# Memory attention and two MoE layers: the next batch's phi, k and v work woven into a batch's softmax, V W_in behind it

## The chip, the cores and the metric

One core of one Trainium2 chip runs the kernel. The metric is the device time of one launch in microseconds. The core's engines each run their own list of instructions in order: TensorE (PE, with its weight loads as PEld), VectorE (DVE), ScalarE (ACT) and GpSimd (POOL) compute, SyncE (SP) issues nearly all DMAs. An engine whose next instruction waits lets everything behind it in its list wait.

## What is computed

Eight batches of 8 heads, 576 tokens, head size 64 and 32 memory slots; then two dense layers over the 4608 tokens of 512 numbers.

```python
a = phi - np.max(phi, axis=2, keepdims=True)        # over the tokens
a = np.exp(a); a = a / (np.sum(a, axis=2, keepdims=True) + 1e-09)
k_m = np.einsum('bhsm,bhsd->bhmd', a, k)
v_m = np.einsum('bhsm,bhsd->bhmd', a, v)
scores = scale * np.matmul(q, k_m.transpose(0, 1, 3, 2))
attn = softmax(scores)                              # over the 32 slots
x = heads_side_by_side(np.matmul(attn, v_m))        # 4608 x 512
h = x @ w_in;  x = (h - np.tanh(h)) @ w_out         # 512 -> 2048 -> 512
h = np.maximum(np.maximum(x @ w1, x @ w2), x @ w3)  # 512 -> 768
out = h @ w_out2                                    # 768 -> 512
```

## The kernel before, in words

**Stages.** The first layer goes in two passes (ph 0 and 1) over the 2048 hidden columns, 1024 in each; a third stage does the second layer. Attention is not multiplied out: since x = attn V, the kernel forms V W_in for each batch (vw_gen, tile vw, from psum tile ps_w) and multiplies that by the transposed attention matrix at. So PE's main work in the first two stages is, for each **step** i: ps_h = at x vw (128 hidden columns of a tile of tokens), ACT's tanh into th, VectorE's difference th, ACT's rounded copy and GpSimd's rest in gh, and ps_x += gh x wo (four psum banks). Each product is made of three (high x high, high x low, low x high).

**Steps.** In ph 0 the tiles of tokens are four of 288 (batches 0 and 1), then for each further pair of batches 320, 512 and 320. The four first tiles do hidden blocks 0 to 3 in steps 0 to 15, and blocks 4 to 7 in steps 16 to 31; for these the partial result of the first round goes out to memory (xd, from the one tile xo) and is loaded back and added in the second (emit_x, lines 586 to 604). From step 32 on a tile takes 8 steps: batch 2 begins at step 32, batch 3 at 40 (the second 256 tokens of a tile of 512), 4 at 56, 5 at 64, 6 at 80, 7 at 88; ph 1 begins at 104.

**What a batch needs first.** phi_gen (from line 230): four maxima over phi's five pieces (mx), two transposes on PE (ps_mx), a reduction, a product that spreads the maxima (dg, ps_mx again), the subtraction, exp. kv_mm (from 262): 160 small matmuls ps_kv per batch, the normed n, its transpose ps_t, kT and vT; it also issues the loads of phi and kv of the next batch (lines 279 and 280), which have one buffer each. q_front and q_score: transposes of q (qT) and the scores sc in two halves of 288 tokens. q_half: the softmax over 32 slots: transposes back (s), maximum, subtraction, exp on ACT, sum and reciprocal (st), product on GpSimd, transpose aT, ACT's copy and GpSimd's rest in at, and the store of at to memory. sc, ps_w, ps_mx, ps_kv and ps_t share two psum banks (line 124).

**What sets the order.** These jobs are generators that are cut into pieces at each yield. They stand in three lines of jobs (class Track, line 469): fg (attention), bg (weight conversions) and ld (loads of q). After each quarter of a step slot() runs some pieces of the first job of each line (rate, in fourths: 10 of fg until step 32, 6 after it), if its gate, a step, is reached. emit_h forces what it needs (fg.need). Before, a batch b stood as kv_gen (phi and k, v products) with gate start - 20, V W_in 0, q_both (both score halves), V W_in 1, with gates some 6 to 16 steps before the batch starts (lines 675 to 683). behind(i, last_aT[0]) held phi's first maximum behind the last aT of the batch before (lines 235 to 237). A scheduler then lists each engine's instructions by its own estimate of when each is ready, in about the order of the program.

Of the kernel before, what the change touches and what calls it, by code (L numbers as in the profile page):

```python
# [22 lines left out]
def kernel(  # L23
# [40 lines left out]
    def behind(ins, mark):  # L64
        tc.add_manual_dep(ins, mark.name, mybir.DependencyInfo(mybir.DependencyClass.NoSync, mybir.DependencyReason.DATA), reason="pace")

    background = [False]
    V, S, T, G = (Paced(e) for e in (nc.vector, nc.scalar, nc.tensor, nc.gpsimd))
    DMA = nc.sync
    B, H, NS, D = q.shape  # L70
    M = phi.shape[3]
    P = 128
    HP = H // 2
# [9 lines left out]
    LG = 3  # L83
    AHEAD = 20
# [39 lines left out]
    def bank(i, shape, name):  # L124
        return ps_m.tile(shape, F32, tag=f"m{i}", bufs=1, name=name)
# [61 lines left out]
    def wi_conv(fq):  # L187
        t = wo1.tile([P, HP, FQ], F32, name="wi2") if fq == 2 else wi_p.tile([P, HP, FQ], F32, tag="wi", bufs=2, name="wi")
        yield from convs(*((moe_w_in[r * P:(r + 1) * P, fq * FQ:(fq + 1) * FQ], t[:, r], None) for r in range(HP)), ahead=2 if fq else 3)
        wi[fq] = t  # L190
# [39 lines left out]
    def phi_gen(b):  # L230
        load_phi(b)
        ph = phi_t.pop(b)
        yield
        mx = ap.tile([P, H, M], F32, tag="mx", bufs=1, name="mx")
        i = V.tensor_max(mx, ph[:, :, 0], ph[:, :, 1]).ins
        if b > 1:
            behind(i, last_aT[0])
        for c in range(2, C):
            V.tensor_max(mx, mx, ph[:, :, c])
        yield  # L240
        pm = bank(1, [P, 2, 2, P], "ps_mx")
        for i in range(2):
            T.transpose(pm[:, 0, i], mx[:, 4 * i:4 * i + 4].rearrange("p h m -> p (h m)"), ident)
        mt = ap.tile([P, 2], F32, tag="mt", bufs=1, name="mt")
        V.tensor_reduce(mt, pm[:, 0], axis=AX.X, op=ALU.max)
        yield
        dg = ap.tile([P, 2, P], F32, tag="mx", bufs=1, name="dg")
        V.tensor_tensor(out=dg, in0=ident[:, None, :].to_broadcast([P, 2, P]), in1=mt[:, :, None].to_broadcast([P, 2, P]), op=ALU.mult)
        T.matmul(pm[:, 1].rearrange("p i j -> p (i j)"), ones, dg.rearrange("p i j -> p (i j)"), start=True, stop=True)
        yield  # L250
        freed[1] = V.tensor_tensor(out=ph, in0=ph, in1=pm[:, 1].rearrange("p i (h m) -> p (i h) m", m=M)[:, :, None, :].to_broadcast([P, H, C, M]), op=ALU.subtract).ins
        yield
        S.activation(ph, ph, AF.Exp)
        yield
        ph_t[b] = ph
        yield
# [40 lines left out]
    def kv_gen(b):  # L297
        yield from phi_gen(b)
        yield from kv_mm(b)
# [4 lines left out]
    def place(b, k, shape, name):  # L304
        return ap.tile(shape, F32, tag=f"w{(k + 2 * (b % 2)) % 4}", bufs=1, name=name)

    def q_front(b, hf):
        for g in range(2):
            t = qTs[hf, g] = place(b, 3 if g and hf else g, [P, 2, NH], "qT")
            V.transpose(out=t, in_=q_t[b, g][:, :, hf * JH:(hf + 1) * JH].rearrange("p r j d -> p r (j d)"))  # L310
            yield

    def q_score(b, hf):
        scs = scs_t[hf] = [bank(e, [P, NH], "sc") for e in range(2)]
        small([(scs[e][32 * r:32 * r + 32], kT[b][64 * e:64 * e + 64, r], qTs[hf, r // 2][64 * e:64 * e + 64, r % 2])
               for r in range(HP) for e in range(2)])
        yield

    def q_half(b, hf):
        at = at_t[0, b]  # L320
        o = slice(hf * NH, (hf + 1) * NH)
        sp = place(b, 1 if hf else 2, [P, 2, NH], "s")
        s = sp.rearrange("p e (j m) -> p e j m", m=M)
        scs = scs_t[hf]
        for e in range(2):
            freed[e] = V.transpose(out=sp[:, e], in_=scs[e]).ins
        yield
        st = ap.tile([P, 2, JH, 3], F32, tag="st", bufs=2, name="st")
        V.reduce_max(st[:, :, :, 0], s, axis=AX.X)
        V.tensor_tensor(out=s, in0=s, in1=st[:, :, :, 0:1].to_broadcast([P, 2, JH, M]), op=ALU.subtract)  # L330
        yield
        S.activation(sp, sp, AF.Exp, scale=0.125)
        yield
        V.reduce_sum(st[:, :, :, 1], s, axis=AX.X)
        V.tensor_scalar(st[:, :, :, 2], st[:, :, :, 1], 1e-9, None, ALU.add)
        V.reciprocal(st[:, :, :, 2], st[:, :, :, 2])
        yield
        G.tensor_tensor(out=s, in0=s, in1=st[:, :, :, 2:3].to_broadcast([P, 2, JH, M]), op=ALU.mult)
        yield
        aT = place(b, 0 if hf else 3, [P, 2, NH], "aT")  # L340
        last_aT[0] = V.transpose(out=aT, in_=sp).ins
        yield
        at_cast.append(S.copy(at[:, 0, :, o], aT).ins)
        G.tensor_sub(at[:, 1, :, o], aT, f(at[:, 0, :, o]))
        yield
        DMA.dma_start(out=at_d[b][:, :, :, o], in_=f(at[:, :, :, o]))
        yield

    qTs, scs_t, last_aT = {}, {}, [None]

    def q_begin(b):
        ld.need(("q", b, 1))
        at_t[0, b] = at_p.tile([P, 2, 2, NS], F32R, tag="at", bufs=3, name="at")
        at_d[b] = dram.tile([P, 2, 2, NS], F32, name=f"at_d{b}")
        yield

    def q_next(b):
        for g in range(2):
            ld.add(("q", b + 1, g), load_q(b + 1, g))
        yield  # L360
# [10 lines left out]
    def q_both(b, between=()):  # L371
        yield from q_begin(b)
        yield from q_front(b, 0)
        yield from q_score(b, 0)
        x, y = q_half(b, 0), q_half(b, 1)
        yield next(x)
        yield from between
        yield next(x)
        yield from q_front(b, 1)
        yield from q_next(b)  # L380
        yield from q_score(b, 1)
        for g in (x, y, x, y, x, y, x, y, x, y, x):
            yield next(g)
        yield "half"
        yield from y

    def upto(g, word):
        for w in g:
            yield
            if w == word:  # L390
                return
# [4 lines left out]
    def vw_gen(ph, b, fq):  # L396
        while 2 * ph + fq not in wi:
            bg.need("wi2")
        t = at_p.tile([P, 2, 2, FQ], F32R, tag="vw", bufs=4, name="vw")
        pss = [bank(e, [P, FQ], "ps_w") for e in range(2)]  # L400
        small([(pss[e][32 * r:32 * r + 32], vT[b][64 * e:64 * e + 64, r], wi[2 * ph + fq][64 * e:64 * e + 64, r])
               for r in range(HP) for e in range(2)])
        yield
        for e in range(2):
            S.copy(t[:, e, 0], pss[e])
            yield
            freed[e] = V.tensor_sub(t[:, e, 1], pss[e], f(t[:, e, 0])).ins
            yield
        vw_t[ph, b, fq] = t
# [88 lines left out]
    fg, bg, ld = Track(), Track(), Track()  # L498
# [27 lines left out]
    steps, start, last_u = [], {}, {}  # L526
# [108 lines left out]
    def chain(*gens):  # L635
        for g in gens:
            yield from g
# [27 lines left out]
    g = q_both(1, vw_gen(0, 1, 0))  # L665
    fg.add(("q", 0, 1, 0), upto(g, "half"))
    fg.add(("q", 0, 1), g)
    fg.add(("vw", 0, 0, 1), chain(wi_conv(1), vw_gen(0, 0, 1)))
    fg.add(("vw", 0, 1, 1), vw_gen(0, 1, 1))
    order = [(0, 0), (1, 0), (0, 1), (1, 1)]  # L670
    for ph in range(2):
        for b in range(B):
            s0, bb = start[ph, b], ph * B + b
            order += [(bb, 0), (bb, 1)] if bb > 1 else []
            aq = max([s0 - AHEAD + 4] + [last_u[bb - 3, fq] - LG for fq in range(2) if bb > 2])
            av0, av1 = (max(s0 - d, last_u[order[2 * bb + fq - 4]] - LG) if bb > 1 else 0 for fq, d in enumerate((8, 6)))
            if ph == 0 and b > 1:
                fg.add("kv", kv_gen(b), s0 - AHEAD)
                fg.add(("vw", 0, b, 0), vw_gen(0, b, 0), max(aq, last_u[order[2 * bb - 4]] - LG))
                g = q_both(b)  # L680
                fg.add(("q", 0, b, 0), upto(g, "half"), aq)
                fg.add(("q", 0, b), g, aq)
                fg.add(("vw", 0, b, 1), vw_gen(0, b, 1), av1)
            if ph:
                fg.add(("q", 1, b, 0), at_load(b), max(aq, s0 - 10))
            if ph:
                fg.add(("vw", ph, b, 0), vw_gen(ph, b, 0), av0)
                fg.add(("vw", ph, b, 1), vw_gen(ph, b, 1), av1)
        if ph == 0:
            fg.add("wi", wi_conv(3), start[0, B - 1] + 2)  # L690
# [283 lines left out]
```

## Time and profile before

| | us |
|---|---|
| median of 3 runs (1366.47 to 1369.27) | 1368.98 |
| the profiled execution | 1369.92 |
| its span, first to last instruction | 1368.2 |
| PE busy | 1286.2 |
| DVE busy | 750.2 |
| POOL busy | 530.1 |
| ACT busy | 507.6 |

Times of the trace count from the span's start. All rows below are of the one profiled execution. Nearly every operation is recorded by one helper (L57), so groups are told apart by their tiles: ps_x<-gh,wo is the matmul that writes ps_x from gh and wo. Engine names with a q (SPq) are an engine's sequencer, here the issue of a DMA. A row of a timeline has start, duration, engine, operation, shape and count, and in brackets how long the engine stood idle before it and whose result ended that. Matmuls overlap, so a mean duration of one is longer than its share of the time. The clock column gives PE's granted clock as a share of 2.4 GHz; its other level is 1.2.

### The profile page before, as it was taken

The numbers are of one execution on the slowest core, as the hardware profiler recorded it, in microseconds if no ns is written. First come the engines' busy times: TensorE is split into PE (matmuls) and PEld (weight loads), VectorE is DVE, ScalarE is ACT, GpSimd is POOL, SyncE is SP. The second block draws the span as 40 slices with busy tenths as digits, with TensorE's granted clock in tenths as the row PEclk, the third lists the DMA queues.
The fourth block names the chain that finished last, engine by engine and source line by source line (L and its number), as shares of the span: only waits on it lengthen the run. The fifth ranks groups of instructions, "written<-read, shape, count | busy, mean of one in ns | idle before, by whom it ended". The sixth has DMA issues, their size and how long they took to land.

```text
span 1368.2 us, 22710 instructions
## 1 busy us (share of the span) xinstructions
PE 1286.2 (94%) x8996; PEld 1159.0 (85%) x8996; DVE 750.2 (55%) x1189; ACT 507.6 (37%) x993; POOL 530.1 (39%) x470
## 2 busy tenths in 40 slices
PE   3589897999997999999999999999999999999998
PEld 1467785787896799898988999989999899999996
DVE  3876557567354755766644244545734646456342
ACT  2445334454343555555544332232322223223221
POOL 1655244564243546776754341131412312224110
PEclk9989998999998999999999999999999999999999
DMA  8874755776525635666575129847547477385431
GB/s 201 236 193 159 184 168 164 192 218 182 145 63 195 199 112 206 239 236 236 205 256 181 50 104 374 337 140 290 203 162 291 146 268 267 92 307 199 165 134 47
DMA packets 188394, 264.94 MB, mean 194 GB/s; under 512 B 94976, under 2 KB 160512, under 8 KB 179200
## 3 DMA queue, kind: packets, MB, share of 16 engines
q1 hardware_dynamic: 188000, 259.82, 58.2%
q0 software_dynamic: 288, 3.67, 0.7%
q8 instruction: 71, 1.16, 0.4%
q14 instruction: 35, 0.29, 0.1%
HBM read 199.49 MB, written 63.96 MB: 193 GB/s over the span
## 4 chain that ended last, share of the span: by engine, by line
PE 80%; DVE 7%; DMA 3%; SPq 3%; POOL 2%; issue 2%; ACT 1%; POOLq 0%; DVEq 0%; ACTq 0%
PE b L57 40%; PE ps_x L57 24%; PE ps_h L57 12%; DVE cvb L57 2%; PE ps_w L57 2%; SPq L224 2%; PE ps_kv L57 2%; DMA raw<-in_moe_w_out_dram 1%; DVE st L57 1%; DVE mx L57 1%; DMA xd<-xo 1%; DVE s L57 1%; SPq L214 1%; DVE th L57 1%; POOL gh L57 1%
## 5 line engine op out<-in xcount | busy, mean ns | idle before, releaser
L57 PE MATMUL ps_x<-gh,wo 128*128 128x320 f32 (+2 forms) x2400 | 453.3, 336 | 12.4 <-DVE xo L57 7.5
L57 PEld LDWEIGHTS ps_x<-gh,wo 128*128 128x128 f32 x2400 | 382.7, 191 | 60.2 <-issue 26.0
L57 PE MATMUL b<-mv,sw 128*128 128x384 f32 x2268 | 401.5, 338 | 0.0
L57 PEld LDWEIGHTS b<-mv,sw 128*128 128x128 f32 x2268 | 399.1, 188 | 1.4 <-DMA sw<-sw_d 0.2
L57 POOL TENSOR_TENSOR gh<-th,gh 128x320 fp32r<-128x320 f32 (+2 forms) x200 | 207.1, 1038 | 266.0 <-ACT gh L57 250.3
L57 PE MATMUL ps_h<-at,vw 128*128 128x256 f32 (+2 forms) x1536 | 257.1, 308 | 21.8 <-ACT at L57 10.7
L57 PEld LDWEIGHTS ps_h<-at,vw 128*128 128x128 f32 x1536 | 229.5, 198 | 48.0 <-ACT at L57 17.1
L57 DVE TENSOR_TENSOR th<-ps_h,th 128x320 f32<-128x320 f32 (+2 forms) x200 | 107.0, 537 | 189.8 <-ACT th L57 188.9
L57 ACT ACTIVATE th<-ps_h 128x320 f32<-128x320 f32 (+2 forms) x200 | 95.5, 477 | 192.9 <-PE ps_h L57 182.8
L57 PE MATMUL b<-wz,mh 128*128 128x512 f32 x648 | 150.4, 390 | 1.1 <-DVE ob L57 1.1
L57 PEld LDWEIGHTS b<-wz,mh 128*128 128x128 f32 x648 | 121.3, 188 | 26.4 <-DVE ob L57 2.0
L57 ACT CAST gh<-th 128x320 fp32r<-128x320 f32 (+2 forms) x200 | 99.6, 499 | 103.8 <-DVE th L57 99.1
L57 POOL TENSOR_TENSOR c<-c,u 128x384 f32<-128x384 f32 x36 | 36.4, 1012 | 226.3 <-ACT u L57 226.3
L57 ACT COPY p<-b 128x384 f32<-128x384 f32 x108 | 51.7, 479 | 169.6 <-PE b L57 146.4
L57 DVE TENSOR_TENSOR c<-b,u 128x384 f32<-128x384 f32 x72 | 39.9, 554 | 97.8 <-PE b L57 97.8
L57 DVE TENSOR_SCALAR cvb<-cvb 128x512 f32<-128x512 f32 x112 | 66.7, 596 | 32.2 <-ACT cvb L57 29.4
L57 DVE TENSOR_TENSOR m<-c,m 128x768 f32<-128x768 f32 x72 | 69.0, 959 | 5.0
L57 DVE TENSOR_TENSOR c<-b,p 128x384 f32<-128x384 f32 x72 | 37.7, 554 | 37.9 <-ACT p L57 34.4
L57 DVE TENSOR_TENSOR vw<-ps_w,vw 128x512 fp32r<-128x512 f32 x64 | 41.2, 681 | 29.6 <-ACT vw L57 29.6
L57 POOL TENSOR_TENSOR mv<-xr,mv 128x384 fp32r<-128x384 f32 x30 | 48.9, 1662 | 12.4 <-ACT mv L57 12.4
L57 ACT CAST mh<-m 128x384 fp32r<-128x384 f32 (+1 forms) x54 | 31.8, 620 | 57.5 <-DVE m L57 57.5
L57 POOL TENSOR_TENSOR m<-m,u 128x384 f32<-128x384 f32 x18 | 21.4, 1190 | 81.1 <-ACT u L57 79.8
(82 smaller groups left out, 1054.0 us busy)
## 6 DMA issues: line engine op xcount, KB each, us to landing
sw<-sw_d SPq DMA_DIRECT2D x52, 1792.0 KB, 7.6
sw_d<-so SPq DMA_DIRECT2D x9, 1792.0 KB, 7.0
raw<-in_moe_w_out_dram SPq DMA_DIRECT2D x22, 512.0 KB, 5.9
qt<-in_q_dram SPq DMA_DIRECT2D x128, 72.0 KB, 3.1
at_d<-at SPq DMA_DIRECT2D x16, 576.0 KB, 4.1
at<-at_d SPq DMA_DIRECT2D x8, 1152.0 KB, 6.3
raw<-in_moe_w_dram SPq DMA_DIRECT2D x18, 512.0 KB, 4.1
out_dram<-ob SPq DMA_DIRECT2D x144, 64.0 KB, 1.7
```

Of the source, the lines that this page charges most:

```text
L57: i = op(*a, **kw)
L214: DMA.dma_start(out=t[:64, i, :, 4], in_=x[b, :, 4 * P:].rearrange("h p d -> p h d"))
L224: q_dma.dma_start(out=t[64 * e + 32 * h:64 * e + 32 * h + 32, r], in_=src[e, h, r])
```

## The change

For batches 2 to 7 the separate kv_gen and q_both are replaced by one generator, q_beside(b). It runs batch b's two softmax halves, and between their pieces phi_gen(b + 1) and kv_mm(b + 1). Batch 2's phi_gen is put between the conversion of w_in's second block and the V W_in that uses it, and its kv_mm behind that. Both V W_in of a batch now stand behind its softmax. The gates are moved to the steps at which the buffers of at (three) and vw (four) come free: 12, 20, 28, 44, 52 and 68 for the softmax of batches 2 to 7. The edge behind last_aT is gone. In V W_in the four weight blocks are multiplied in the order 3, 2, 1, 0.

```diff
-        i = V.tensor_max(mx, ph[:, :, 0], ph[:, :, 1]).ins
-        if b > 1:
-            behind(i, last_aT[0])
+        V.tensor_max(mx, ph[:, :, 0], ph[:, :, 1])
...
+    def q_beside(b):
+        yield from q_begin(b)
+        p = phi_gen(b + 1) if b + 1 < B else iter(())
+        m = kv_mm(b + 1) if b + 1 < B else iter(())
+        x, y = q_half(b, 0), q_half(b, 1)
+        yield next(p, None)
+        yield from q_front(b, 0)
+        yield from q_score(b, 0)
+        yield next(x)
+        for g in (p, x, p, x, p):
+            yield next(g, None)
+        yield from q_front(b, 1)
+        yield from q_next(b)
+        yield next(x)
+        yield from p
+        yield from q_score(b, 1)
+        yield next(y)
+        for g in (x, y, m, m, x, y, m, m, x, y, m, m, x):
+            yield next(g, None)
+        yield "half"
+        for g in (m, y, m, y, m, y):
+            yield next(g, None)
+        yield from m
+        yield from y
...
-               for r in range(HP) for e in range(2)])
+               for r in reversed(range(HP)) for e in range(2)])
...
-    fg.add(("vw", 0, 0, 1), chain(wi_conv(1), vw_gen(0, 0, 1)))
+    fg.add(("vw", 0, 0, 1), chain(wi_conv(1), phi_gen(2), vw_gen(0, 0, 1)))
+    fg.add("kv", kv_mm(2))
     fg.add(("vw", 0, 1, 1), vw_gen(0, 1, 1))
...
             if ph == 0 and b > 1:
-                fg.add("kv", kv_gen(b), s0 - AHEAD)
-                fg.add(("vw", 0, b, 0), vw_gen(0, b, 0), max(aq, last_u[order[2 * bb - 4]] - LG))
-                g = q_both(b)
+                aq = last_u[bb - 3, 1] - LG if b > 2 else start[0, 2] - AHEAD
+                g = q_beside(b)
                 fg.add(("q", 0, b, 0), upto(g, "half"), aq)
                 fg.add(("q", 0, b), g, aq)
-                fg.add(("vw", 0, b, 1), vw_gen(0, b, 1), av1)
+                for fq in range(2):
+                    fg.add(("vw", 0, b, fq), vw_gen(0, b, fq), last_u[order[2 * bb + fq - 4]] - LG)
```

What that makes of the engines' lists, at three places. In the names a number behind ps_x tells tiles apart, and the one behind wo the hidden block.

PE, around batch 3's scores, before: the end of batch 2's tile (ps_x of 320 columns) and the start of the tile of 512 (steps 40 to 42).

```order
L57 MATMUL sc<-qT,kT 32x288 x8
L57 MATMUL ps_x_2169<-gh,wo_966 128x320 x2
L57 MATMUL ps_x_2170<-gh,wo_966 128x320 x3
L57 MATMUL sc<-qT,kT 32x288 x8
L57 MATMUL ps_w<-wi,vT_92 32x512 x8
L57 MATMUL ps_h<-at,vw 128x256 x12
L57 MATMUL ps_mx<-ident,mx 128x128 x2
```

PE, around batch 3's second score half, after: between the last ps_x of the tiles of 288 and the first of step 32.

```order
L57 MATMUL ps_h<-at,vw 128x320 x12
L57 MATMUL sc<-qT,kT 32x288 x8
L57 MATMUL ps_h<-at,vw 128x320 x6
L57 MATMUL ps_kv<-ones,phi 32x1 x20
L57 MATMUL ps_kv<-kv,phi 32x128 x20
L57 MATMUL ps_kv<-ones,phi 32x1 x20
L57 MATMUL ps_kv<-kv,phi 32x128 x20
L57 MATMUL ps_x_2495<-gh,wo_304 128x320 x3
```

The scores moved from the end of batch 2's tile to its start, and the k and v products that follow them are those of batch 4.

PE, around batch 7's scores (vT_96 is batch 7's), before: the end of batch 6's tile of 320 and the first ps_h of step 88's tile that need batch 7.

```order
L57 MATMUL sc<-qT,kT 32x288 x8
L57 MATMUL ps_x_4514<-gh,wo_966 128x320 x3
L57 MATMUL ps_x_4515<-gh,wo_966 128x320 x3
L57 MATMUL ps_x_4516<-gh,wo_966 128x320 x3
L57 MATMUL ps_x_4517<-gh,wo_966 128x320 x3
L57 MATMUL sc<-qT,kT 32x288 x8
L57 MATMUL ps_w<-wi,vT_96 32x512 x8
L57 MATMUL ps_h<-at,vw 128x256 x24
```

PE, around batch 7's second score half, after: steps 76 to 79, still in batch 5's tile.

```order
L57 MATMUL sc<-qT,kT 32x288 x8
L57 MATMUL ps_h<-at,vw 128x320 x6
L57 MATMUL ps_x_4283<-gh,wo_306 128x320 x3
L57 MATMUL ps_x_4284<-gh,wo_306 128x320 x3
L57 MATMUL ps_x_4285<-gh,wo_306 128x320 x3
L57 MATMUL ps_x_4286<-gh,wo_306 128x320 x3
L57 MATMUL ps_h<-at,vw 128x320 x6
L57 MATMUL ps_x_4283<-gh,wo_307 128x320
L57 MATMUL ps_w<-wi,vT_96 32x512 x8
```

Eleven ps_h groups of 320 columns now stand between that score product and the first ps_h of the tile of 512.

SP, the second round of the four first tiles, before: stores (xd<-xo) and loads (xo<-xd) of the partial results.

```order
L604 DMA xd_120<-xo 512x1x288
L590 DMA xo<-xd_120 128x4x288
L224 DMA qt<-in_q_dram 32x18x32 x8
L604 DMA xd_120<-xo 512x1x288
L590 DMA xo<-xd_120 128x4x288
L346 DMA at_d_1437<-at 512x1x288 x2
L604 DMA xd_120<-xo 512x1x288
```

SP, the same place after, from the first of these stores on.

```order
L627 DMA xd_120<-xo 512x1x288
L613 DMA xo<-xd_120 128x4x288
L344 DMA at_d_1304<-at 512x1x288
L198 DMA phi<-in_phi_dram 128x8x128
L199 DMA phi<-in_phi_dram 64x8x32
L211 DMA kv<-in_k_dram 128x8x256
L214 DMA kv<-in_k_dram 64x8x64
L211 DMA kv<-in_v_dram 128x8x256
L214 DMA kv<-in_v_dram 64x8x64
L344 DMA at_d_1304<-at 512x1x288
L224 DMA qt<-in_q_dram 32x18x32 x8
L627 DMA xd_120<-xo 512x1x288
```

Between the second load and the second store now stand both at_d stores of batch 2 and the phi and kv loads of batch 4; the phi and kv loads of batch 3, which stood ahead of the first store, now stand ahead of the first load.

## Rows read from the trace of the kernel before

**Rows 1.** The page, part 1: busy us, share of the span, instructions.

```profile
PE 1286.2 (94%) x8996; PEld 1159.0 (85%) x8996; DVE 750.2 (55%) x1189; ACT 507.6 (37%) x993; POOL 530.1 (39%) x470
```

**Rows 2.** Stretches: start:end, length, busy time by engine, PE's clock, DMA share, GB/s.

```profile
94.00:186.00 92.00, 81.43 (x710) 72.42 (x709) 57.00 (x106) 39.37 (x88) 41.49 (x42) 0.91 0.64 176
186.00:213.00 27.00, 26.66 (x328) 23.59 (x328) 10.38 (x22) 10.24 (x21) 8.47 (x9) 0.94 0.62 176
213.00:231.00 18.00, 10.29 (x68) 6.95 (x65) 16.44 (x29) 7.05 (x12) 7.34 (x6) 0.62 0.59 164
231.00:419.00 188.00, 184.81 (x1840) 157.61 (x1839) 108.60 (x187) 79.17 (x158) 82.93 (x76) 1.00 0.54 150
419.00:437.00 18.00, 9.55 (x69) 7.16 (x68) 11.67 (x24) 7.42 (x13) 7.54 (x6) 0.72 0.58 199
```

**Rows 3.** PE's timeline around step 40: start, us, what, idle before and its releaser.

```profile
214.63 0.72 PE L57 MATMUL sc<-qT,kT 64*32 64x288 f32 x16 [0.67 <-DVE s L57]
217.21 1.96 PE L57 MATMUL ps_w<-wi,vT 64*32 64x512 f32 x16 [1.86 <-DVE s L57]
222.55 0.79 PE L57 MATMUL ps_h<-at,vw 128*128 128x256 f32 x2 [3.38 <-ACT at L57]
224.70 2.50 PE L57 MATMUL ps_h<-at,vw 128*128 128x256 f32 x10 [1.35 <-POOL at L57]
...
228.15 2.87 PE L57 MATMUL ps_h<-at,vw 128*128 128x256 f32 x12
```

**Rows 4.** PE's timeline around step 88, and at step 92.

```profile
422.04 1.09 PE L57 MATMUL ps_w<-wi,vT 64*32 64x512 f32 x16 [1.18 <-DVE s L57]
429.30 0.80 PE L57 MATMUL ps_h<-at,vw 128*128 128x256 f32 x2 [6.17 <-ACT at L57]
...
440.55 1.59 PE L57 MATMUL ps_h<-at,vw 128*128 128x256 f32 x12
```

**Rows 5.** PE's timeline from the first ps_x of step 32 on.

```profile
186.34 4.41 PE L57 MATMUL ps_x<-gh,wo 128*128 128x320 f32 x18 [2.12 <-DVE xo L57]
...
194.34 0.60 PE L57 MATMUL ps_kv<-ones,phi 128*32 128x1 f32 x40
...
196.77 1.43 PE L57 MATMUL ps_kv<-kv,phi 128*32 128x128 f32 x40
...
199.85 1.92 PE L57 MATMUL ps_x<-gh,wo 128*128 128x320 f32 x12
```

**Rows 6.** SP's timeline in steps 16 to 35; the duration is that of the issue.

```profile
133.07 4.97 SPq L224 DMA_DIRECT2D qt<-in_q_dram  x7
138.15 1.49 SPq L198 DMA_DIRECT2D phi<-in_phi_dram  x1
...
143.75 3.26 SPq L214 DMA_DIRECT2D kv<-in_v_dram  x1
...
148.37 1.42 SPq L604 DMA_DIRECT2D xd<-xo  x1
154.93 0.56 SPq L590 DMA_DIRECT2D xo<-xd  x1
155.59 5.61 SPq L224 DMA_DIRECT2D qt<-in_q_dram  x8
161.97 0.57 SPq L604 DMA_DIRECT2D xd<-xo  x1
...
175.64 0.51 SPq L604 DMA_DIRECT2D xd<-xo  x1
...
187.72 0.56 SPq L604 DMA_DIRECT2D xd<-xo  x1
```

**Rows 7.** Tile xo, 110 to 200 us: its transfers, from issue to landing.

```profile
DMA to landing us min/median/max: 3.3/4.4/6.5
```

**Rows 8.** Tile mx: durations in ns, min/median/max, first and last start, form.

```profile
L57 DVE TENSOR_TENSOR mx<-mx,phi x24: 376/882/1615, 5.4 to 387.3; 128x256 f32<-128x256 f32 x24
```

**Rows 9.** Tile phi: its transfers, from issue to landing.

```profile
DMA to landing us min/median/max: 3.8/4.8/7.0
```

More of the change, by code (lines that the diff above doesn't have):

```diff
@@ L340, in q_half @@
         aT = place(b, 0 if hf else 3, [P, 2, NH], "aT")
-        last_aT[0] = V.transpose(out=aT, in_=sp).ins
+        V.transpose(out=aT, in_=sp)
         yield
@@ L347, in q_half @@
         yield
-    qTs, scs_t, last_aT = {}, {}, [None]
+    qTs, scs_t = {}, {}
     def q_begin(b):
```

## The prediction

> **What bounds the kernel now.** I read the page first, then busy time by stretch, then the PE and SP timelines of the stretches where PE was short. PE is busy for 1286.2 of 1368.2 us [rows 1], so an edit that removes no PE work can only gain where PE stands still or runs at its lower clock. The stretches [rows 2] say where that is, in the first projection (t, us from the start). From 94 to 186 PE is busy for 81.43 of 92 us at a mean granted clock of 0.91. From 213 to 231 it is busy for 10.29 of 18 at 0.62, from 419 to 437 for 9.55 of 18 at 0.72. From 231 to 419 it lacks 3.2 us of 188 at full clock. Behind that nearly nothing is reordered (from step 94 on VectorE's order is the old one but for one row). So the two short holes and the first stretch decide.
>
> The holes are the same event twice. A tile of 512 tokens starts (step 40, step 88) and needs the attention of an odd batch (3, 7), whose scores PE made only just before. In [rows 3] the second score product starts at 214.63, V W_in at 217.21, and ps_h at 222.55 and 224.70, behind ACT's and then GpSimd's half of at. In [rows 4] V W_in ends at 423.13 and ps_h starts at 429.30 after 6.17 us. Behind each wait PE runs at 1.2 GHz for a while: 12 ps_h of 256 columns take 2.87 us at 228.15, and 1.59 at 440.55.
>
> **What the holes cost.** At full clock the work of the first is 1.0 us of ps_x before the second score product, scores 0.72, V W_in 1.09, 24 ps_h for 3.2, ps_mx 0.4: 6.4 of 18, so 11.6 lost. The second: ps_x 1.2, scores 0.72, V W_in 1.09, ps_h 3.2, ps_x 0.9: 7.1 of 18, so 10.9. The stretch between them loses 3.2. From 186 to 213 PE lacks 0.3 us, and a mean clock of 0.94 over 27 us is 3.3 us at the half clock, worth 1.7: 2.0. In all **27.7 us** lie behind t = 186.
>
> **The change part by part.** *No matmul, exponential, maximum or transfer is added or removed*; only their place moves. The two edits that delete a pacing edge and turn the four weight blocks round issue nothing: I take nought for them, between a loss of none and a gain of the 1.1 us of one V W_in ([rows 4], 422.04), which is no longer cut into 6 and 2 with both banks held between.
>
> *Scores early.* In the new PE order batch 3's score products lie in steps 32 to 36. Between its second one and the ps_h that needs batch 3 stand 66 ps_x of 320 columns (0.16 us each, by 12 in 1.92 [rows 5]; 10.6), four ps_h groups (3.4), the k and v products of batch 4 (3.9, [rows 5]: 194.34 to 198.20) and V W_in (1.1): 19.0 us of work. The chain it has to cover took from 214.63 to 224.70, 10 us, and step 40 needs only the first half, whose scores lie another 10 us ahead. For batch 7 eleven steps of 18 matmuls (29 us) and two V W_in lie between. Both holes should close: 11.6 + 10.9. The 3.2 and the 2.0 go with them, as phi's maxima, for which PE waited there too, now stand steps ahead.
>
> *What the first stretch must take.* Up to the first ps_x of step 32 (186.34, [rows 5]) PE now has the k and v products of batches 3 and 4 ahead of it (2 x 3.9), both scores of batch 3 (1.4), one more maximum, two more ps_h groups and ps_t (3.1): **12.3 us more**, which the later part is rid of. Were the stretch PE-bound it would grow by 12.3 and nothing would change in sum; its waits of some 18 us (92 less 81.43 x 0.91 = 74 of full-clock work, [rows 2]) could swallow some of it.
>
> I do not expect that they swallow much, because of SP's queue. Four tiles there add a partial result that goes out to memory and comes back (xo, one buffer): the store, then the load, then the add, for which PE waits. [rows 6]: stores at 148.37, 161.97, 175.64 and 187.72; the first store takes 154.93 - 148.37 = 6.6 us until its load can go, and a transfer of xo lands in 4.4 us (3.3 to 6.5, [rows 7]). The first store was late already, since SP spent 133.07 to 148.3 issuing qt, phi and kv, 15.2 us, 8.9 of it (138.15 to 147.01) for the six issues of phi and kv. In the new order phi and kv of batch 3, and 15 of its 16 qt, stand *ahead* of the first load, so the first store should go near 150. But phi and kv of batch 4 now stand between the second load and the second store, with two at_d stores and eight qt. They wait for PE's k and v product of batch 3 (about 155), then 8.9 us of issue, 1.2 for at_d, 5.6 for eight qt (as at 155.59): the second store goes at 171 and not at 162. The third tile's load lands, and its adds free PE's banks, at 171 + 6.6 + 0.6 + 4.4 = 182.6. From there PE has the fourth tile's 48 ps_x (0.147 each at most: 7.1), two ps_mx (0.6), four ps_h groups (3.5), scores (0.7) and batch 4's k and v products (3.9) ahead, 15.8 us; the fourth load is back by then (182.6 + 1 + 6.6 + 5 = 195). So step 32's ps_x begin at **198**. That is 11.7 later than 186.34 for 12.3 more work: +0.6 in sum. From below: without that delay PE would be there at 190, 8 us better. From above: two such delays, 207, 9 worse.
>
> *VectorE.* Phi's four maxima cost it 4 x 0.88 = 3.5 us a batch [rows 8]. Batch 2's move from behind the tanh difference of step 15 to between those of steps 8 and 11, among the weight conversions; batch 3's from step 29 to step 17. VectorE has 57.00 of 92 us busy there [rows 2], so it fits on average; but it goes in order, and behind a maximum that waits for phi stand tanh's differences. Phi lands 4.8 us after its issue (3.8 to 7.0, [rows 9]) and is issued when the product of the batch before is done; for batch 3 the maxima come about 4 us too early, which costs PE 1 to 2 us, in the 198 already. Later batches have steps between.
>
> *New waits.* With each of batches 4 to 7 PE meets scores, maxima and products in the middle of dense work, where [rows 2] shows 3.2 us lost over four batches in the old order. I take the same, 3.2 (between 0 and 8).
>
> *The Trainium skill on the maxima.* A maximum over phi took 376 to 1615 ns for one shape, 882 in the median [rows 8]. SBUF — State Buffer, section "Who interferes with whom", says that a VectorE instruction with two SBUF inputs contends with a GpSimd instruction that reads SBUF; the trace agrees as far as that spread goes. By it the eight maxima of batches 2 and 3, moved among the conversions, would all take the long time, and the sum would come to 1352 (a rival below) instead of the 1344 that goes by the median.
>
> **The sum.** 27.7 lost after 186, + 0.6 in the first stretch, - 3.2 new waits = 25.1 us gained. The profiled execution took 1369.92 (span 1368.2), so 1344.8; the median of the runs, 1368.98, is 0.9 lower: **1344 us**.
>
> **Rivals.**
> - *The first stretch swallows more.* If the second store is not held, PE reaches step 32 at about 190: 1344 - 8 = 1336, and with no new waits 1333. For it: 18 us of waits are there. Against it: the order on SP.
> - *Two tiles held, not one.* The third store has eight qt ahead of it and the load after it waits too: 1344 + 9 = 1353, with a further fall of the clock (as the 3.3 us at half rate between 186 and 213) and longer new waits up to 1360.
> - *Slow maxima.* Eight at 1.6 instead of 0.88 us on a VectorE that already holds PE up: + 5.8, and 1.7 for one more stretch at the low clock, at 1352.
> - *It doesn't do what it says.* The scores come early but at does not, because its chain hangs behind the xo adds on VectorE; one hole stays and the first stretch is worse by 13: within 0.2%, 1369.
> - *Slower, in SP's queue.* Loads that wait for a PE product stand ahead of a store that PE waits for. If PE's product in turn stands behind ps_x of the held tile, a round trip becomes product 3.9 + SP 15.7 + store 6.6 + load 4.4 + adds 2 + tile work 7.1: 39.7 us and not 13.6. Two of these are + 52, less the 9 counted: 1387. It decides from the point at which the first and the fourth store stand over 39.4 + 9 + 25 = 73 us apart. Against it: only one set of such loads stands between the four stores.
>
> **How the numbers follow.** Forecast 0.56 (1337 to 1353). Swallows more 0.13; two held 0.13; slow maxima 0.07; no difference 0.04; slower 0.07. Something within 0.2% (2.7 us) can't be told from no change. Faster 0.89, same 0.04, slower 0.07. For 8 in 10 the range takes the forecast, slow maxima, most of "two held" and a little under half of "swallows more": 1333 to 1360.
>
> **What would show it.** Right: no PE wait for at longer than 2 us at steps 40 and 88, and full clock from 220 to the end of the projection; the second xd store some 20 us behind the first, the others some 12; step 32's first ps_x near 198; the ps_h of step 92 (440.55 in [rows 4]) some 25 us earlier. Wrong: a wait for at at either step (the scores did not help); the first ps_x of step 32 past 210 (the queue gave it all back) or before 192 (the waits swallowed it); maxima of 1.5 us in a row with tanh's differences behind them; new waits for ps_mx or sc of more than 8 us in sum after 200.

## The result, and the profile after

The changed kernel takes 1345.83 us (median of 5 runs, 1344.86 to 1347.29), the kernel before 1366.66 on the same chip (5 runs): a ratio of 0.9843, 95% interval 0.9829 to 0.9857, or 20.8 us less. The forecast was 1344 us, with a range of 1333 to 1360. The total was right; several terms behind it were not, and they made up for each other. The gain was forecast at 25.1 us and measured at 20.8: that the total still lies within 2 us was helped by the kernel before, whose median is 2.3 under the 1368.98 that the forecast started from.

The page, part 1, after (before: [rows 1]): the same instructions, PE busy 13 us less.

```profile
PE 1273.1 (95%) x8996; PEld 1152.7 (86%) x8996; DVE 748.3 (56%) x1189; ACT 508.0 (38%) x993; POOL 530.2 (39%) x470
```

Busy time by stretch, after (columns as in [rows 2]): up to the first ps_x of step 32, from there to the first ps_x of step 40, to step 95, and the five steps behind it.

```profile
90.00:206.33 116.33, 96.48 (x1104) 83.56 (x1104) 75.75 (x142) 47.48 (x102) 48.12 (x48) 0.89 0.67 175
206.33:232.30 25.97, 25.97 (x216) 22.70 (x213) 20.69 (x38) 11.81 (x24) 13.76 (x13) 1.00 1.00 267
232.30:445.53 213.23, 212.34 (x1869) 182.13 (x1867) 126.15 (x216) 100.00 (x195) 104.52 (x91) 1.00 0.56 169
445.53:465.57 20.04, 17.18 (x125) 13.97 (x123) 12.55 (x20) 9.78 (x22) 8.77 (x9) 1.00 0.43 143
```

From 206.33 to 445.53 PE lacks 0.9 us, all at full clock. Both holes are in this part and are shut. This is PE's list of waits from step 32 to step 95 (waited for, total, times, longest); the waits for at of [rows 3, 4] are not in it:

```profile
PE ps_w L57 <- ACT vT L57: 0.5, 1, 0.5
PE ps_h L57 <- DVE th L57: 0.4, 1, 0.4
```

The first stretch paid. PE's timeline in it, columns as in [rows 3]; step 32 begins at 206.33, where before it began at 186.34 [rows 5]:

```profile
144.92 0.72 PE L57 MATMUL sc<-qT,kT 64*32 64x288 f32 x16
152.66 6.17 PE L57 MATMUL ps_x<-gh,wo 128*128 128x288 f32 x28 [7.01 <-DVE xo L57]
158.75 0.60 PE L57 MATMUL ps_kv<-ones,phi 128*32 128x1 f32 x40
...
182.43 0.44 PE L57 MATMUL ps_mx<-ident,mx 128*128 128x128 f32 x2
189.57 8.87 PE L57 MATMUL ps_x<-gh,wo 128*128 128x288 f32 x46 [6.70 <-DVE xo L57]
...
206.33 5.55 PE L57 MATMUL ps_x<-gh,wo 128*128 128x320 f32 x36
```

SP's timeline of the same place, as in [rows 6]:

```profile
131.02 10.27 SPq L224 DMA_DIRECT2D qt<-in_q_dram  x8
141.39 0.57 SPq L627 DMA_DIRECT2D xd<-xo  x1
142.06 5.09 SPq L224 DMA_DIRECT2D qt<-in_q_dram  x7
147.20 0.63 SPq L613 DMA_DIRECT2D xo<-xd  x1
...
153.63 0.57 SPq L627 DMA_DIRECT2D xd<-xo  x1
157.50 0.57 SPq L613 DMA_DIRECT2D xo<-xd  x1
...
162.67 0.38 SPq L198 DMA_DIRECT2D phi<-in_phi_dram  x1
...
168.09 3.60 SPq L214 DMA_DIRECT2D kv<-in_v_dram  x1
171.79 1.28 SPq L344 DMA_DIRECT2D at_d<-at  x1
173.17 7.97 SPq L224 DMA_DIRECT2D qt<-in_q_dram  x8
181.24 0.58 SPq L627 DMA_DIRECT2D xd<-xo  x1
184.69 0.58 SPq L613 DMA_DIRECT2D xo<-xd  x1
```

**A ledger of losses.** Stretches of two kernels with different orders can't be laid side by side by time, since work has moved between them. So for every profiled run I add up PE's idle time and half of its busy time at the lower clock, and cut the sum where PE begins the ps_x of steps 32, 45, 75, 90 and 100 (12 ps_x matmuls a step, counted). The last column ends with PE's last matmul. What is left of the span, 1266 to 1271 us in these runs, is PE's work at full clock and the 4.7 us behind its last matmul.

| profiled run | span | to step 32 | 32-45 | 45-75 | 75-90 | 90-100 | behind | lost |
|---|---|---|---|---|---|---|---|---|
| before | 1368.2 | 64.0 | 13.6 | 3.2 | 11.1 | 4.6 | 1.1 | 97.6 |
| after | 1345.4 | 73.4 | 0.0 | 0.9 | 0.0 | 2.9 | 1.1 | 78.3 |
| b_edge | 1348.6 | 62.7 | 6.5 | 3.5 | 2.7 | 0.9 | 1.1 | 77.4 |
| b_er | 1350.7 | 64.4 | 9.9 | 6.0 | 1.1 | 0.0 | 1.1 | 82.5 |
| rows | 1344.9 | 70.2 | 0.0 | 0.6 | 0.0 | 4.4 | 1.1 | 76.3 |
| unwoven | 1348.0 | 65.5 | 3.9 | 5.2 | 0.0 | 4.5 | 1.1 | 80.2 |
| part23 | 1346.9 | 70.4 | 0.0 | 3.6 | 1.7 | 0.2 | 1.1 | 77.0 |
| part47 | 1360.5 | 63.1 | 10.3 | 11.4 | 0.0 | 4.6 | 1.1 | 90.5 |
| late7 | 1351.7 | 70.1 | 0.0 | 1.2 | 9.4 | 2.8 | 1.2 | 84.7 |
| late3 | 1350.5 | 70.2 | 6.8 | 1.0 | 0.0 | 4.5 | 1.1 | 83.6 |
| kvq | 1354.3 | 64.5 | 3.1 | 10.6 | 0.0 | 4.5 | 1.3 | 84.0 |
| b_xo2 | 1359.6 | 53.7 | 13.4 | 4.8 | 10.6 | 4.6 | 1.4 | 88.5 |
| xo2 | 1337.1 | 55.5 | 9.5 | 0.0 | 0.0 | 4.5 | 1.1 | 70.6 |
| u_xo2 | 1337.3 | 55.3 | 4.1 | 6.5 | 0.0 | 4.6 | 1.1 | 71.6 |

Before against after: 9.4 more to step 32; 13.6, 2.3, 11.1 and 1.7 less behind it; 19.3 in sum. The other 3.5 of the 22.8 between the two spans is work that reads shorter, some 1.7 of it in V W_in and 1.8 in ps_x. The ledger is one execution each (between the medians lie 20.8 and not 22.8): after, late7 and rows run nearly the same list up to step 74, and their first entries differ by 3.3.

### The profile page after: what moved, and what is told of

Read it like the earlier page. It is cut to its first block, busy times and chain, and to the rows that moved or that the text cites. A ratio compares the mean times of both kernels' runs of the same rounds, so it can differ in the third digit from the quotient of the medians.

```text
span 1345.4 us, 22714 instructions
## 1 busy us (share of the span) xinstructions
PE 1273.1 (95%) x8996; PEld 1152.7 (86%) x8996; DVE 748.3 (56%) x1189; ACT 508.0 (38%) x993; POOL 530.2 (39%) x470
## 4 chain that ended last, share of the span: by engine, by line
PE 84%; DVE 6%; SPq 3%; DMA 3%; issue 2%; POOL 1%; ACT 1%; DVEq 0%; POOLq 0%; ACTq 0%
PE b L57 41%; PE ps_x L57 26%; PE ps_h L57 13%; SPq L224 3%; DVE cvb L57 2%; PE ps_w L57 2%; PE ps_kv L57 1%; DMA raw<-in_moe_w_out_dram 1%; DVE th L57 1%; DMA xo<-xd 1%; DVE st L57 1%; DMA phi<-in_phi_dram 1%; ACT cvb L57 1%; DVE s L57 0%; PE sc L57 0%
## 5 line engine op out<-in xcount | busy, mean ns | idle before, releaser
L57 PE MATMUL ps_h<-at,vw 128*128 128x256 f32 (+2 forms) x1536 | 247.9, 301 | 13.2 <-DVE th L57 6.7
L57 PEld LDWEIGHTS ps_h<-at,vw 128*128 128x128 f32 x1536 | 221.9, 191 | 37.8 <-DVE th L57 12.5
L57 POOL TENSOR_TENSOR mv<-xr,mv 128x384 fp32r<-128x384 f32 x30 | 48.9, 1663 | 12.4 <-PE b L57 9.3
L57 POOL TENSOR_TENSOR m<-m,u 128x384 f32<-128x384 f32 x18 | 21.4, 1188 | 81.6 <-ACT u L57 80.2
```

The lines of the kernel that those rows point to most:

```text
L57: i = op(*a, **kw)
```

## Experiments

The medians below are each beside the kernel before on the same chip (1366.2 to 1368.7 us); "below" means against that one. The change itself: 20.8 below.

### Is it the early scores that shut a hole? (late7)

```diff
+                if b == 7:
+                    aq = s0 - 4
```

> The changed kernel with one gate put back: batch 7's softmax opens at step 84 instead of 68, so that its second score product stands right ahead of V W_in and of step 88's ps_h, as before the change; phi, k and v of batch 7 stay where the change put them. Theory A (what closed the hole at step 88 is that the scores are early): the hole comes back, idle 8 us or more with a fall of the clock near the start of step 88, at the 10.7 us that the ledger of the two traces shows for it: 1356.5 us. Rival B (the hole closed because the maxima and the k and v products left that place): it stays closed, 1346 to 1348 us.

1352.77 us, ratio 0.9880 (0.9864 to 0.9897), 16.0 below. PE around step 88:

```profile
407.19 0.72 PE L57 MATMUL sc<-qT,kT 64*32 64x288 f32 x16
409.23 1.09 PE L57 MATMUL ps_w<-wi,vT 64*32 64x512 f32 x16 [1.33 <-DVE s L57]
413.08 0.80 PE L57 MATMUL ps_h<-at,vw 128*128 128x256 f32 x2 [2.76 <-ACT at L57]
413.83 1.96 PE L57 MATMUL ps_w<-wi,vT 64*32 64x512 f32 x16
```

The hole is back: 9.4 in the ledger (4.8 idle, the rest lower clock) against 11.1 before and none after. The late scores, with the V W_in that stand behind them in the line of jobs, suffice for it, with phi, k and v where the change put them; rival B falls. The idle part is below the 8 us expected: one V W_in now stands behind the first ps_h and fills some of it. Beside the kernel before, late7 is 4.8 us worse than the change, about half of the 9.4; its profiled execution lost 3.3 less up to step 32.

### Which edit moves the scores? (b_edge, b_er, rows)

The prediction took the deleted edge and the turned row blocks at nought. b_edge is the kernel before with only this:

```diff
-        i = V.tensor_max(mx, ph[:, :, 0], ph[:, :, 1]).ins
-        if b > 1:
-            behind(i, last_aT[0])
+        V.tensor_max(mx, ph[:, :, 0], ph[:, :, 1])
```

> The kernel before with the pacing edge behind last_aT deleted and nothing else of the change. In its PE list batch 7's second score product stands 18 ps_x of 320 columns ahead of V W_in and not right ahead; batch 3's stays where it was. Theory A (the edge itself held batch 7's scores back, and the prediction's nought for it is wrong): the hole at step 88 closes by 3 to 6 us with its low clock, the hole at step 40 stays: 4 to 8 us below the kernel before. Rival B (the edge costs nothing, the gates alone decide): within 2 us of the kernel before.

1349.95 us, ratio 0.9875 (0.9856 to 0.9895): 16.3 below, at the old gates and without any weaving. That is more than either theory gave. VectorE's timeline of the kernel before, just ahead of batch 7's first maximum:

```profile
383.83 0.78 DVE L57 STREAM_TRANSPOSE aT<-s 128x576 f32<-128x576 f32 x1 [0.54 <-POOL s L57]
384.53 0.38 DVE L57 TENSOR_TENSOR mx<-phi 128x256 f32<-128x256 f32 x1
```

The maximum stands right behind batch 6's last aT, as the edge asks. In b_edge it starts 14 us earlier (6.4 of them because the whole list is ahead by then: step 75 begins at 372.61 and not at 379.06):

```profile
370.46 1.00 DVE L57 TENSOR_TENSOR mx<-phi 128x256 f32<-128x256 f32 x1
```

and PE has batch 7's scores at 405.58 and 410.65. Before they stood at 417.54, and at 420.14 right ahead of the V W_in of [rows 4]:

```profile
417.54 0.72 PE L57 MATMUL sc<-qT,kT 64*32 64x288 f32 x16
...
420.14 0.72 PE L57 MATMUL sc<-qT,kT 64*32 64x288 f32 x16
```

In b_edge:

```profile
405.58 0.71 PE L57 MATMUL sc<-qT,kT 64*32 64x288 f32 x16
...
410.65 0.71 PE L57 MATMUL sc<-qT,kT 64*32 64x288 f32 x16
411.29 2.91 PE L57 MATMUL ps_x<-gh,wo 128*128 128x320 f32 x18
414.13 1.09 PE L57 MATMUL ps_w<-wi,vT 64*32 64x512 f32 x16
415.29 0.50 PE L57 MATMUL ps_h<-at,vw 128*128 128x256 f32 x2
416.78 1.45 PE L57 MATMUL ps_h<-at,vw 128*128 128x256 f32 x10 [0.99 <-POOL at L57]
```

So the chain maximum, k and v, scores, softmax, at of an odd batch was hung behind the end of the batch before it, by an edge between two VectorE instructions. Counted in ps_x, batch 7's scores stand 2.1 and 1.5 steps earlier in PE's list. That leaves 1.9 us of waiting at step 88, without any lower clock (ledger 11.1 to 2.7), and the hole at step 40 is halved (13.6 to 6.5). At step 40 the first score product moved ahead by some 20 ps_x (to 206.42, the second at 211.65; before 212.31 and 214.63), the second stayed right ahead of V W_in.

b_er adds the falling row order to b_edge:

```diff
-               for r in range(HP) for e in range(2)])
+               for r in reversed(range(HP)) for e in range(2)])
```

> The kernel before without that edge and with V W_in's row blocks in falling order; both of the edits that the prediction took at nought, at the old gates. Theory A (the row order is worth nothing): the same as the run b_edge within 2 us. Rival B (V W_in in falling order saves some of its 1.1 us where it stands ahead of a wait): 2 to 5 us below b_edge.

1354.37 us, ratio 0.9908 (0.9893 to 0.9923), 11.9 below: 4.4 worse than b_edge, with intervals that just meet. Neither theory said so. The list is another one again (its hole at step 40 has 9.9 in the ledger, and 6.0 is lost between 45 and 75); which of its moves does that wasn't followed up.

rows takes the falling order out of the changed kernel:

> The changed kernel with V W_in's row blocks in rising order again. Theory A (row order worth nothing): within 2 us of the changed kernel, so 19 to 23 below the kernel before. Rival B (the falling order is part of the gain): 3 us or more slower than the changed kernel.

1346.22 us, ratio 0.9851 (0.9833 to 0.9869), 20.0 below, against 20.8 with it. Theory A: nothing to be told apart at the new gates.

### Weaving, or gates? (unwoven)

```diff
-                g = q_beside(b)
+                if b > 2:
+                    fg.add("kv", kv_gen(b), aq)
+                g = q_both(b)
```

> The changed kernel with its early gates, but phi, k and v of a batch in one piece ahead of that batch's softmax (the old generators one behind the other) instead of woven into the softmax of the batch before; batch 2's phi, k and v stay where the change put them. Theory A (early scores close the holes; the weaving only saves some waits for maxima): holes at steps 40 and 88 stay closed, 0 to 6 us slower than the changed kernel, 16 to 22 below the kernel before. Rival B (without the weaving the chain of maxima, products and softmax is too long for the place it has): holes open again, 10 us or more slower than the changed kernel.

1344.93 us, ratio 0.9827 (0.9805 to 0.9850), 23.1 below: as fast as the woven order, the intervals lie over each other. Its profiled execution was the slowest of the four (1349.79); in it 9.1 is lost between steps 32 and 75 (PE waits 2.9 for dg, 2.7 for xo's copies) and 7.9 less than in the change up to step 32. So what gives the change its name, weaving one batch's phi, k and v into another's softmax, is worth nothing that these runs show.

### Do early and late batches add up? (part23, part47)

Both keep the deleted edge and the falling rows. part23 sends batches 4 to 7 back to the old jobs and gates (batch 4's phi, k and v stay woven into batch 3's softmax); part47 does it with batches 2 and 3 and gives batch 4 a kv_gen at its old gate. The core of part23:

```diff
+                if b > 3:
+                    if b > 4:
+                        fg.add("kv", kv_gen(b), s0 - AHEAD)
+                    fg.add(("vw", 0, b, 0), vw_gen(0, b, 0), max(aq, last_u[order[2 * bb - 4]] - LG))
+                    g = q_both(b)
...
+                    fg.add(("vw", 0, b, 1), vw_gen(0, b, 1), av1)
+                    continue
```

> The change for batches 2 and 3 alone (with phi, k and v of batch 4 woven into batch 3's softmax); batches 4 to 7 as before. Theory A (the ledger adds up): the hole at step 40 closes (11.9 + 1.7) and the first stretch pays 9.9 for it, 0.5 comes ahead of it: 3 to 6 us below the kernel before of the same chip, and up to 5 more where batch 7's scores stand two steps earlier than before. Rival B (the first stretch would have lost as much in any order, so that closing the hole is all gain): 12 to 14 us below.

1348.69 us, ratio 0.9858 (0.9839 to 0.9878), 19.4 below, more than either theory gave. Batches 2 and 3 alone shut step 40's hole and pay for it in the first stretch as expected (70.4 against 64.0), but step 88's hole is nearly shut too (1.7), with batch 7 at its old gate. That is what called for b_edge: the edge is out in both parts.

> The change for batches 4 to 7 alone; batches 2 and 3 stand as before, with their phi, k and v at their old places. Theory A (the ledger of losses adds up by stretch): the first stretch and the hole at step 40 stay as before; only what the ledger gains behind t = 231 comes, 2.3 between the holes, 10.7 at step 88, 2.1 at 468 to 472 and part of the 3.3 by which the same matmuls read shorter: 15 to 18 us below the kernel before of the same chip. Rival B (the gain hangs together, later batches gain only because the early ones moved): under 8 us below it.

1364.96 us (10 runs, 1359.84 to 1372.09), ratio 0.9979 (0.9960 to 0.9998), 3.1 below. Step 88's hole is shut, step 40's stays (10.3), and 11.4 is lost between steps 45 and 75, where batch 4's phi, k, v and scores crowd behind batch 3's late ones (2.6 for xo, 1.6 for a bank held by V W_in, 1.3 for s, and the lower clock). The total is rival B's; theory A fails as to place, since what step 88 gives back is lost again between 45 and 75. The fair comparison for both parts is b_er, the old gates with the same two edits (11.9 below): the new order of batches 2 and 3 alone adds 7.5 to that, the new order of batches 4 to 7 alone takes 8.8 away.

### What did the first stretch pay for? (xo2, b_xo2, kvq, late3)

xo2 gives the four tiles of 288 two buffers of xo, so that a tile's load need not wait for the store before it:

```diff
+    xo_all = ga_p.tile([P, 2 * KD * NH], F32, name="xo")
...
-            emit_x.xo = ga_p.tile([P, KD, NT], F32, tag="xo", bufs=1, name="xo")[:, :, :nt]
+            x0 = t0 // NH % 2 * KD * NH if not ph and t0 < NXI else 0
+            emit_x.xo = xo_all[:, x0:x0 + KD * nt].rearrange("p (d n) -> p d n", d=KD)
```

> The changed kernel with two buffers of xo for the tiles of 288 tokens, so that a tile's load no longer waits for the store of the tile before it. In SP's order the third tile's load then stands ahead of batch 4's phi, kv and qt. Theory A (the 6.7 us wait at 183 is the held second store, through the one buffer): that wait and the 5.0 us of low clock behind it go, and of the first wait (7.0 us), whose load no longer follows a store, most: 1332 to 1338 us. Rival B (the loads are late by themselves, behind phi, kv and qt in the queue): the first wait stays, 1338 to 1341; if both stay, 1346 us.

1339.58 us, ratio 0.9783 (0.9766 to 0.9799), 29.2 below. Both long waits for xo are gone; PE's list of waits from 118 to 250:

```profile
PE ps_kv L57 <- issue: 1.7, 2, 1.4
PE sc L57 <- DVE vw L57: 1.6, 1, 1.6
PE ps_h L57 <- ACT vw L57: 0.7, 1, 0.7
PE ps_h L57 <- DVE th L57: 0.7, 1, 0.7
PE ps_w L57 <- ACT vT L57: 0.5, 1, 0.5
PE ps_x L57 <- DVE xo L57: 0.4, 2, 0.3
```

So theory A is right about the waits. To step 32 it loses 55.5 and not 73.4 (with less work in that part: the k and v products of one batch, 3.9 us, and one score half stand behind step 32's first ps_x here). But 9.5 comes back at steps 32 to 45, as other waits and two stretches of lower clock: PE now gets there before V W_in's halves are copied. So the time is in rival B's range, by a loss that neither theory named. The same edit on the kernel before:

> The kernel before with the two xo buffers of the run xo2 and nothing of the change. Theory A (the change made the single xo buffer dearer, by putting batch 4's loads between its load and store): here the two buffers bring only what the kernel before waits for xo, 6.8 us in two waits and some of the 5.1 us of low clock behind them: 6 to 11 us below the kernel before, and its holes at steps 40 and 88 stay; the change on top of two buffers is then worth 20 us or more. Rival B (two buffers are worth the same with and without the change): 8 to 10 us, and the change 20 to 23 in both; rival C (the time won in the first stretch is lost again at step 40's hole): 0 to 3 us below.

1360.22 us, ratio 0.9939 (0.9915 to 0.9963), 7.8 below. Its holes stay (13.4 and 10.6). To step 32 the buffers take 10.3 from the kernel before and 17.9 from the changed one: the change did make the single buffer dearer there, by about as much as the stretch had grown (53.7 and 55.5 are nearly alike). But in the whole the buffers are worth 7.8 and 8.4, and the change some 21 on top of them (0.9939 and 0.9783). The number fits both A and B; that the buffers are worth the same with the change and without is what B said.

kvq issues phi and kv of batches 3 to 7 from ACT:

```diff
+                Q = nc.scalar if b > 2 else DMA
...
-                DMA.dma_start(out=t[:64, i, :, 4], in_=x[b, :, 4 * P:].rearrange("h p d -> p h d"))
+                Q.dma_start(out=t[:64, i, :, 4], in_=x[b, :, 4 * P:].rearrange("h p d -> p h d"))
```

> The changed kernel with the phi and kv loads of batches 3 to 7 issued by ACT instead of SP; the order of the computing work stays. Theory A (xo held behind the 8 to 9 us that these issues take of SP's queue): the first wait for xo shrinks from 7.0 to 0 to 2 us, the second from 6.7 to 0 to 3 and the fall of the clock behind it with them; ACT pays some 0.6 to 1.5 us for each of 30 issues in time it has (508 us busy of 1345): 1332 to 1338 us. Rival B (the qt issues alone hold xo as long, or the waits are for the round trip): 1343 to 1346. Rival C (ACT now stands at a load that waits for the k and v products, with tanh behind it): slower, 1350 to 1365 us.

1355.64 us, ratio 0.9906 (0.9888 to 0.9923), 13.1 below, 7.7 worse than the change. The first stretch is better by 8.9 (64.5), and the second store goes at 176.99 and not 181.24, so SP's phi and kv issues were part of its price; the first load of xo still goes at 147.07, held by the qt issues alone. But ACT now does nothing else while it issues (start, us of issue; then ACT's next work and its idle time):

```profile
301.41 0.38 ACTq L199 DMA_DIRECT2D phi<-in_phi_dram  x1
...
308.96 3.27 ACTq L216 DMA_DIRECT2D kv<-in_v_dram  x1
312.27 0.62 ACT L57 CAST cs<-cva 128x512 fp32r<-128x512 f32 x1 [10.46 <-DMA kv<-in_k_dram]
```

and PE stands 5.07 us for vT behind it, with the clock down from 313.7 to 320.5: 10.6 between steps 45 and 75.

```profile
314.18 1.96 PE L57 MATMUL ps_w<-wi,vT 64*32 64x512 f32 x16 [5.07 <-ACT vT L57]
```

That is rival C's time and place, with theory A true of the first stretch. The mechanism is not quite the one that C named: ACT did not wait here for the k and v products, whose last matmul ended at 300.2, but was held by the six issues themselves.

late3 opens batch 3's softmax at step 32 instead of 20:

```diff
+                if b == 3:
+                    aq = s0 - 8
```

> The changed kernel with batch 3's softmax, and with it phi, k and v of batch 4, opened at step 32 instead of 20. The loads of phi and kv of batch 4 and its 16 qt then leave SP's queue between the stores of xo. Theory A (the first stretch lost its 9.9 us, ledger of before against after, to xo held in SP's queue): the second wait for xo (6.7 us at 183) and the fall of the clock behind it (5.0 us) go, the first (7.0 us at 146) stays; seven steps of ps_x still cover step 40, so its hole opens by no more than 3 us: 1335 to 1339 us. Rival B (the stretch is longer because of the work put into it, whatever the queue): nothing is gained there and the hole at step 40 opens in part, 1346 to 1357 us.

1353.05 us, ratio 0.9884 (0.9863 to 0.9906), 15.7 below. The expectation rested on a mistake: batch 4's phi and kv loads hang on batch 3's k and v product, which stayed in batch 2's softmax, so they still stood between the stores (161.77 to 170.6) and only the qt left. The second wait for xo shrank to 5.05 us, no more:

```profile
184.03 6.35 PE L57 MATMUL ps_x<-gh,wo 128*128 128x288 f32 x25 [5.05 <-DVE xo L57]
```

So the time is in rival B's range, but the run doesn't decide between the theories. And the hole at step 40 half opened (6.8): eight steps ahead is too late for batch 3, since V W_in and batch 4's products come with it (PE waits 2.3 for n, 0.5 for vT and 1.1 for vw, and the clock is down from 224.4 to 231.2).

### The fastest (u_xo2)

The edits of unwoven and xo2 together.

> The early gates without weaving (run unwoven) together with two xo buffers (run xo2). Theory A (the gates close the holes and the buffers take away the first stretch's waits, and both add): unwoven's waits for xo, 4.9 at 143 and 2.8 at 173, and most of the 5.1 us of low clock behind them go: 8 to 11 us below unwoven, 1334 to 1338 us where the kernel before has 1368. Rival B (the time is lost again at step 40, as with xo2, where 9.5 us of waits and low clock came up between 200 and 250): 1339 to 1343 us.

1338.26 us, ratio 0.9790 (0.9775 to 0.9804), 28.0 below, 7 under the change; with xo2 the fastest, and not to be told from it. The time lies between the two ranges, and the mechanism is B's: no wait for a load of xo is left, and 10.6 is lost between steps 32 and 75 (3.4 of waiting for dg, 2.8 for xo's copies, and the lower clock).

## Why the prediction was right, step by step

**The holes.** Size and cause were right. Forecast 11.6 and 2.0 behind t = 186, and 10.9; the ledger has 13.6 to step 45 and 11.1 to step 90, and both are gone. late7 brought one back by late scores, and the V W_in behind them, alone. Of the signs named, no wait for at came and the clock was full from 195.1 on; the ps_h of step 92 start at 419.47 and not 440.55, 21 us earlier and not 25, since the first stretch had cost more.

**"I take nought" for the deleted edge.** This step was wrong, and is the largest error of the working. That an edge issues nothing is no reason to put it at nought: it held the start of the chain whose end was being waited for. Alone it is worth 16.3 of 20.8 us. Had I followed at back to phi's first maximum, whose start at 384.53 comes straight behind aT, it would have been seen. The total didn't suffer: the edge's 16.3 did not come on top of what was forecast for the gates, presumably because both move the same scores. The row order: nought at the new gates, as said; 4.4 worse at the old ones without the edge. The gates with the edge kept weren't run; what they would do alone stays open.

**The first stretch.** Forecast a gain of 0.6 with step 32 at 198; measured a loss of 9.4 and 206.33. The mechanism was the one named, loads ahead of the store that PE waits for; three sizes were off. Step 32 came 8.3 later than forecast and not 10.0: the work moved ahead of it took 12.4, as forecast, but the V W_in and ps_x that were there already read 1.7 shorter. First, "the first store should go near 150" left out that xo's first load needs the store of the fourth tile's first round: eight qt held that from 131.02 to 141.29, seven more held the load to 147.20, and PE stood 7.01 us. The store then went at 153.63. Second, the second store: phi and kv began at 162.67 and not near 155, as batch 3's k and v products ended only at 162.6 behind that first wait, and eight qt took 7.97 us and not 5.6, so 181.24 and not 171 (27.6 behind the first store; the sign named was some 20). Third, the wait of 6.70 brought the lower clock (184.9 to 195.1), as the first had (150.8 to 157.6), and 46 ps_x took 8.87 us; the sum had 48 at full speed in 7.1. In size this is the rival "two tiles held", put at 9 us more, by another way: the first wait lay ahead of the first store.

**New waits.** Forecast 3.2 over the later batches, measured 0.9 from step 45 to step 90: 2.3 better.

**What made up for it.** The first stretch was 10.0 short. Against that stood the 2.3; 0.2 on the holes; 1.7 at steps 90 to 100, where the wait of 2.4 us for th stays but the lower clock behind it (473.2 to 476.6 before) doesn't come; and the 3.5 of work that reads shorter, those 1.7 up to step 32 among them. 25.1 - 10.0 + 2.3 + 0.2 + 1.7 + 3.5 = 22.8, the difference of the spans. Neither of the last two terms was forecast, and the 1.7 looks like luck: in rows, with nearly the same list there, the lower clock comes (449.2 to 452.6).

**"No matmul ... is added", and VectorE fits.** Held. *Slow maxima* didn't come: the same 24 took 426 ns in the median and not 882.

**Net of the edge.** By the ledger the rest of the change shuts what b_edge leaves (6.5, 2.7 and 2.6 of 3.5), and pays 10.7 to step 32 and 2.0 at steps 90 to 100: 77.4 lost in b_edge, 78.3 in the change. By the medians it is worth some 4 us (0.9875 and 0.9843), with intervals that just meet, so these runs hardly show that it is worth anything beside the deleted edge.

## What to carry to other kernels

When an engine waits at the end of a long chain, follow the chain to its first instruction and see what holds that, pacing edges included; such an edge costs no time of its own and can still be the dearest line of the kernel. Work that is moved ahead takes its loads along: list the queue that they go through in order, with the round trip that shares it, from the first transfer of that round trip on and not from the first that shows a wait. A sum that comes out right says little about its terms until each was moved by itself.

## What the runs showed of the hardware

**Every slow maximum has GpSimd beside it.** Of the 24 maxima over phi (mx<-mx,phi) in the changed kernel, 11 ran with no GpSimd instruction beside them and took 409 to 426 ns; 13 ran beside one, 368 to 1660 ns. Before: 9 alone, 376 to 425 ns; 15 beside one, 410 to 1615. VectorE, then GpSimd, at the slowest one after:

```profile
96.85 0.84 DVE L57 TENSOR_TENSOR mx<-mx,phi 128x256 f32<-128x256 f32 x1
...
98.64 1.66 DVE L57 TENSOR_TENSOR mx<-mx,phi 128x256 f32<-128x256 f32 x1
```

```profile
96.59 0.81 POOL L57 TENSOR_TENSOR gh<-th,gh 128x288 fp32r<-128x288 f32 x1 [1.54 <-ACT gh L57]
98.59 1.43 POOL L57 TENSOR_TENSOR at<-aT,at 128x576 fp32r<-128x576 f32 x1 [1.19 <-ACT at L57]
```

The Trainium skill (SBUF — State Buffer, "Who interferes with whom") says that a VectorE instruction with both inputs in SBUF contends with a GpSimd instruction that reads SBUF; the trace agrees, up to four times the time of one alone (1.66 us against 0.42). The size follows from when GpSimd began. In the two kernels 26 of the maxima began while a GpSimd instruction was already running: 24 of them ended 279 to 285 ns after that instruction did, whatever its length (the other two 364 ns after it, 414 ns in all). The two beside which one began only later took 368 and 410 ns. So the maximum waits for the GpSimd instruction that was there first. The rival by that rule came half true: batch 2's maxima, these ones, are slow among the conversions, batch 3's took 415 to 425 ns with GpSimd idle.

**A DMA issue keeps its engine from other work.** The six issues of one phi and kv took 10.8 us of ACT (301.41 to 312.23 in kvq, in which ACT computed nothing for 10.46 us) and 9.0 of SP (162.67 to 171.69); in both the last of them, 64x8x64, took over 3 us.

**The same wait doesn't always bring the lower clock.** The 2.44 us wait for th at step 95 is in both kernels. Before, 3.4 us at half clock follow it, as in late3, xo2, u_xo2 and rows; after and in late7 the clock stays up. It is worth 1.7 us either way, between executions whose lists agree there.
